# Reciprocal row sums spread by column strips of the array in place of row strips

## The chip, the cores and the metric

The kernel runs on one core of a Trainium2 chip. Its time is the device time in microseconds (us) of one launch; the time given for a kernel is the median of its runs. The engines of the core work side by side, each through its own queue in order: TensorE (PE; its weight loads are listed as PEld), VectorE (DVE), ScalarE (ACT), GpSimd (POOL) and SyncE (SP), which issues DMAs. The profile is one execution, recorded by the hardware.

TensorE multiplies a stationary operand of up to 128 rows by 128 columns (loaded by a weight load) with a moving one. In the profile a matmul's shape begins with the part of the array that it uses: `32*128` is a strip of 32 rows by all 128 columns (a row strip), `128*32` or `128*21` a strip of all rows by 32 columns (a column strip), `128*128` the full array.

## The reference

Four layers in a row, each a layer norm, an attention and a residual sum, on one sequence of 2048 rows of 640 numbers in bf16. There are 32 heads of 20. Layers 0 and 2 use weights A and look at a window of 256 rows; layers 1 and 3 use weights B and look at all rows.

```python
S, D, H, Dh, W = 2048, 640, 32, 20, 256
def attention(x, wqkv, wo, mask):
    q, k, v = split(x @ wqkv)                      # each 32 heads x 2048 x 20
    scores = einsum("bhqd,bhkd->bhqk", q, k) * Dh ** -0.5
    scores = where(mask, scores, -1e9)             # A: 0 <= i - j < 256; B: no mask
    o = einsum("bhqk,bhkd->bhqd", softmax(scores), v)
    return merge_heads(o) @ wo

x = A_x
x = x + A(layernorm(x)); x = x + B(layernorm(x))
x = x + A(layernorm(x)); x = x + B(layernorm(x))
```

## The kernel before

The rows are cut into four chunks of 512 queries, and the heads into eight groups of four. A *unit* is one layer, one chunk of queries and one group of four heads (layers 1 and 3 cut some units further by keys). Each head of a group lies on its own 32 partitions, 20 of which are used.

The main loop goes in ticks. In each tick TensorE computes up to three (at times four) banks of scores of 128 keys by 512 queries at L1326, from row strips, since each head has only 32 partitions; ScalarE takes the exponential of all of them in one instruction at L1357; and TensorE multiplies earlier exponentials with the values at L1387, from column strips: the four heads of a group write their 21 columns into four strips of 32 partitions. The 21st column of the values is one, so that the row sums of the softmax come out beside the results. Scores alternate between two sets of banks, so that TensorE writes one while ScalarE reads the other.

All other work (layer norm, projections, output products) is written as generators, which yield shares of cost. A planner (`pump`, `choose`, `advance`) advances them tick by tick, by the credit of the tick and by the unit that first needs their result; this happens when the program is built, so the order on each engine is fixed by the planner's costs and not by the times on the chip. Generators take one of two PSUM banks (`take_m`, `drop_m`), and when the planner reckons that TensorE has had too little to do in a tick (`cool`), it puts in matmuls whose result nobody reads (`unread`, `keep_clock`, `warm_bank`: groups of four of `ident` with `masks`, by column strips at L300). `by_columns` (L300) issues a product as four matmuls, one for each 32 columns of its stationary operand. The transposes of the layer norm at L437 have the same shape of 128 rows by 32 columns.

When a unit ends, its results and row sums are copied out of PSUM (L864), and units go in pairs into a *tail*, `t_tail`, which the planner prefers to all other work. The tail picks the row sums out with `sel4` (L300, 4 columns each), takes reciprocals (L1053), splits each into a high and a low bf16 part (L1057, L1058), transposes both (L1066) and copies them to `rT` (L1071), where a unit has 32 rows: 16 high and 16 low ones, one for each head and block of 128 queries. Then `scaled` spreads them for each unit: four matmuls (L1088), one for each block of 128 queries, whose stationary operand `spread4` has ones where a row belongs to a head. They use the 32 rows of the unit alone, the first unit's rows 0 to 31 and the second's 32 to 63, and all 128 columns. VectorE multiplies the unit's results by the spread (L1092), and with that the bank is free again. In the last tail `fill` adds matmuls of the full array (L1038). `rT` comes from a pool of three buffers; `spread4` is made once, on VectorE, in `other_constants` (L172 to L178).

Of the kernel before, what the change touches and what calls it, by code (L numbers as in the profile page):

```python
# [9 lines left out]
BF16 = mybir.dt.bfloat16  # L10
# [7 lines left out]
P = 128  # L18
# [30 lines left out]
def kernel(  # L49
# [10 lines left out]
    nc = tc.nc  # L60
# [3 lines left out]
    def pool(name, bufs, space=None):  # L64
        kw = {"space": space} if space else {}
        return ctx.enter_context(tc.tile_pool(name=name, bufs=bufs, **kw))

    big = pool("big", 1)
# [10 lines left out]
    rzp = pool("rzp", 3)  # L79
# [14 lines left out]
    ident = big.tile([P, P], BF16, name="ident", tag="ident")  # L94
    nhalf = big.tile([P, 4], F32, name="nhalf", tag="nhalf")
    sel4 = big.tile([P, 4], BF16, name="sel4", tag="sel4")
    spread4 = big.tile([64, 4, P], BF16, name="spread4", tag="spread4")
    masks = big.tile([P, 3, C], BF16, name="masks", tag="masks")

    kts = [big.tile([P, S], BF16, name=f"kt{n}", tag=f"kt{n}") for n in range(3)]  # L100
# [27 lines left out]
    def packed(l, c):  # L128

        return l == 3 and c > 0  # L130

    def load_wop(w, dense):
# [9 lines left out]
        out=ident[:], in_=ident[:], compare_op=ALU.not_equal, fill=1.0,  # L142
# [6 lines left out]
    for m, b, ge in (  # L149
# [6 lines left out]
            out=v, in_=v, compare_op=ALU.is_ge if ge else ALU.is_gt, fill=0.0,  # L156
# [5 lines left out]
    def other_constants():  # L162
        nc.vector.memset(op, 0.0)
        nc.vector.tensor_copy(
            out=sel4[:], in_=ident[:].rearrange("p (j m) -> p j m", j=4)[:, :, DH]
        )

        sp32 = rzp.tile([64, 2, 16], BF16, name="sp32", tag="sp32")
        sp16 = rzp.tile([64, 16], BF16, name="sp16", tag="sp16")
        for u in range(2):  # L170
            r = slice(32 * u, 32 * u + 32)
            nc.vector.tensor_copy(  # L172
                out=sp32[r], in_=ident[r, r].rearrange("p (n r) -> p n r", n=2)
            )
            nc.vector.tensor_tensor(
                out=sp16[r], in0=sp32[r, 0, :], in1=sp32[r, 1, :], op=ALU.add
            )
            nc.vector.tensor_copy(  # L178
                out=spread4[r].rearrange("p q (j m) -> p (q j) m", m=32),
                in_=sp16[r].unsqueeze(2).to_broadcast((32, 16, 32)),  # L180
            )

# [83 lines left out]
    def take_m():  # L266
        while True:
            b = min(mfree, key=mfree.get)
            if mfree[b][0] <= state["tick"]:
                mfree[b] = (1 << 30, 0)  # L270
                return b
            yield ("wait", 1)

    def drop_m(b):
        mseq[0] += 1
        mfree[b] = (state["tick"] + (not state["early"]), mseq[0])
# [19 lines left out]
    def by_columns(out_, lhsT, rhs, start, stop):  # L296

        for j in range(4):
            r = slice(32 * j, 32 * j + 32)
            nc.tensor.matmul(out_[r], lhsT=lhsT[:, r], rhs=rhs, start=start, stop=stop)  # L300
# [343 lines left out]
    def warm_bank(b):  # L644

        if cool() and (
            state["credit"] <= 0.0 or all(task.wake > state["tick"] for task in todo)
        ):
            unread(b)
# [382 lines left out]
    def t_tail(us):  # L1032
        final = us[-1][0:3] == (3, NC - 1, G - 1)

        def fill(count):

            for n in range(count * final):
                nc.tensor.matmul(  # L1038
                    ps[:, 0, :], lhsT=ident[:], rhs=masks[:, 0, :], start=True, stop=True
                )  # L1040

        n = len(us)
        yield ("wait", 2)
        fill(2)
        mb = yield from take_m()
        warm_bank(mb)
        zp = ps[:, mb, 0 : 16 * n]
        for i, (l, c, g, oT) in enumerate(us):
            for qb in range(4):
                a = 16 * i + 4 * qb  # L1050
                by_columns(zp[:, a : a + 4], oT[:, qb * P : (qb + 1) * P], sel4[:], True, True)
        rz = rzp.tile([P, 2, 16], F32, name="rz", tag="rz")[:, 0:n, :]
        nc.vector.reciprocal(out=rz.rearrange("p u r -> p (u r)"), in_=zp)  # L1053
        drop_m(mb)

        hl = rzp.tile([P, 2, 2, 16], BF16, name="hl", tag="hl")[:, 0:n]
        nc.vector.tensor_copy(out=hl[:, :, 0, :], in_=rz)  # L1057
        nc.vector.tensor_tensor(out=hl[:, :, 1, :], in0=rz, in1=hl[:, :, 0, :], op=ALU.subtract)  # L1058
        yield ("pe", 0.25)
        fill(3)  # L1060
        yield ("wait", 2)
        mb = yield from take_m()
        warm_bank(mb)
        rp = ps[0 : 32 * n, mb, :].bitcast(BF16)[:, 0:P]
        for i in range(n):
            nc.tensor.transpose(  # L1066
                out=rp[32 * i : 32 * i + 32], in_=hl[:, i].rearrange("p n r -> p (n r)"),
                identity=ident[:],
            )
        rT = rzp.tile([64, P], BF16, name="rT", tag="rT")  # L1070
        nc.vector.tensor_copy(out=rT[0 : 32 * n], in_=rp)  # L1071
        drop_m(mb)
        yield ("pe", 0.1)
        fill(1)
        yield ("wait", 2 if state["tick"] < last_tick[0] else 1)
        for i in range(n):
            yield from scaled(*us[i], 32 * i, rT, fill)
        if any(packed(l, c) for l, c, g, oT in us):
            yield ("wait", 2)
        for u in us:  # L1080
            yield from settle(*u)

    def scaled(l, c, g, oT, r, rT, fill):
        mb = yield from take_m()
        warm_bank(mb)
        zb = ps[:, mb, :]
        for qb in range(4):
            nc.tensor.matmul(  # L1088
                zb[:, qb * P : (qb + 1) * P], lhsT=spread4[r : r + 32, qb, :],
                rhs=rT[r : r + 32, :], start=True, stop=True,  # L1090
            )
        nc.vector.tensor_tensor(out=oT, in0=oT, in1=zb, op=ALU.mult)  # L1092
        drop_m(mb)
        yield ("pe", 0.3)
        fill(3)

    def settle(l, c, g, oT):
        on = ons[l, c]
        if packed(l, c) and not ((l, c) == (3, NC - 1) and g >= G - 2):
            for j in range(4):  # L1100
                r, a = (4 * g + j) * DH, 0
                while a < DH:
                    b, o = divmod(r + a, P)
                    n = min(DH - a, P - o)
                    nc.sync.dma_start(  # L1105
                        out=on[o : o + n, b, :], in_=oT[32 * j + a : 32 * j + a + n, :]
                    )
                    a += n
            if g == G - 1 or (l, c, g) == (3, NC - 1, G - 3):
                yield ("wait", 8)  # L1110
        ready.add(("tail", l, c, g))
        if (l, c, g) == (3, NC - 1, G - 3):
            push("before_last", t_before_last(), 0, 8.0)
        if g == G - 1:
            while any(("tail", l, c, n) not in ready for n in range(G)):
                yield ("wait", 1)
            need = first_use(l + 1, c, 0) if l < 3 else len(units) + c
            push(("out", l, c), t_out(l, c), need, 9.0)
            if l < 3:
                push_layer(l + 1, c)  # L1120
# [82 lines left out]
    with tc.manual_schedule():  # L1203
        first_ln()
        push_layer(0, 0)
        push("zeros", t_zeros(), 0, 0.0)
        require(("qk", 0, 0, 0))
        other_constants()

        def narrow(u):  # L1210
# [10 lines left out]
        while n < last_layer:  # L1221
            size = 2 if len(tiles) % 2 and narrow(banks[n][0]) else 3
            u = banks[n][0]
            at = placed.setdefault(id(u), [])
            extra = []
            if (
# [3 lines left out]
                kc, j = u.aside[len(at)]  # L1230
# [58 lines left out]
        while ended is None or t < ended + 8:  # L1289
# [3 lines left out]
            if t < len(tiles) or banks:  # L1293
# [9 lines left out]
                for b in cur:  # L1303
                    u = b[0]
# [18 lines left out]
                for n in range(2):  # L1323
                    for i, (u, j, m, b0, subs, first, last, end) in enumerate(cur):
                        for kc, q0, qn, col in subs[n : n + 1]:
                            nc.tensor.matmul(  # L1326
                                sp[:, i, col * P : (col + qn) * P],
                                lhsT=u.k(kc, j), rhs=u.q(j, q0, qn), start=True, stop=True,
# [22 lines left out]
                i = 0  # L1351
                while i < n_b:
                    b0 = cur[i][3]
                    k = i
                    while k < n_b and cur[k][3] == b0:
                        k += 1
                    nc.scalar.activation(  # L1357
                        out=pt[:, i:k, b0 * P :], in_=sp[:, i:k, b0 * P :],
                        func=ACT.Exp, scale=SCALE,
                    )  # L1360
                    i = k
# [9 lines left out]
            for n in range(2 if n_b == 0 or t > closed + 1 else 0):  # L1371
                u = pts[0][3][0] if pts else None
# [11 lines left out]
                for m, (kc, q0, qn, col) in enumerate(subs):  # L1384
                    for _, pg, i, b in group:
                        j = b[1]
                        nc.tensor.matmul(  # L1387
                            op[32 * j : 32 * j + VW, q0 * P : (q0 + qn) * P],
                            lhsT=u.v(kc, j), rhs=pg[:, i, col * P : (col + qn) * P],
                            start=(first and m == 0), stop=(last and m == len(subs) - 1),  # L1390
                            skip_group_check=u.windowed,
                        )
                if end and u.aside:
                    pair = side_done(u)
                    for n, (kc, j) in enumerate(u.aside):
                        nc.tensor.matmul(  # L1396
                            op[32 * j : 32 * j + VW, :], lhsT=u.v(kc, j),
                            rhs=pair[n // 2][:, n % 2, :], start=False,
                            stop=all(jj != j for _, jj in u.aside[n + 1 :]),
# [14 lines left out]
            if t > 0 and masked is not None:  # L1414
                cur_, pt_ = masked
                i = 0
                while i < len(cur_):
                    m, b0 = cur_[i][2:4]
# [4 lines left out]
                    for b in ((3,), (1, 2), (0,))[m] if split else ():  # L1423
                        if b < b0:
# [4 lines left out]
                            out=v, in_=v, compare_op=ALU.is_gt if later else ALU.is_ge, fill=0.0,  # L1429
# [3 lines left out]
                    if split and m != 1:  # L1433
# [5 lines left out]
                            out=pt_[:, i:k, cols], in0=pt_[:, i:k, cols], in1=mv_, op=ALU.mult  # L1439
                        )  # L1440
                    elif m is not None and not split:
# [5 lines left out]
                            out=pt_[:, i:k, cols], in0=pt_[:, i:k, cols], in1=mv_, op=ALU.mult  # L1447
                        )
                    i = k
# [36 lines left out]
```

## Time and profile before

| | |
|---|---|
| median of 3 runs | 2217.34 us (2212.51 to 2220.05) |
| the profiled execution's own time | 2218.73 us |
| its span, first to last instruction | 2217.0 us |
| mean granted clock of TensorE | 0.99 |
| busy: TensorE, ScalarE | 1930.9 us, 2140.9 us |
| busy: VectorE, POOL | 1201.2 us, 482.5 us |

A row of a group of instructions gives line, engine, operation, the tiles written and read, the shapes and the count; then, behind the first bar, the busy time in us and the mean time of one in ns; and behind the second the idle time of the engine just before them in us, with what ended most of it. A row of the timeline gives start and length in us, then engine, line and tiles; rows of the same kind that follow one another are merged, with their count, and idle time before them stands in brackets. A row of waits gives who waited for whom, the sum in us, the number of times and the longest. A row of a stretch of time gives its ends and length, then the busy time and count of instructions of PE, PEld, DVE, ACT and POOL, the mean granted clock, the share of the DMA engines and GB/s. The ends of matmuls are modelled, so that matmuls that run beside or close behind one another overlap in the rows; distances from start to start are the measure.

### The profile page before, as it was taken

How to read it: one execution, taken by the hardware profiler on the slowest of the kernel's cores; microseconds unless marked ns; L12 is line 12 of the kernel's file. 1: busy time of each engine (PE TensorE's matmuls, PEld its weight loads, DVE VectorE, ACT ScalarE, POOL GpSimd, SP SyncE). 2: the span in 40 equal slices, each digit the busy share in tenths (PEclk: the TensorE clock that was granted, in tenths of full speed). 3: DMA queues.
4: the chain of work that ended last, by engine and by line, in shares of the span. 5: the costliest groups of instructions: out<-in, count | busy, mean ns of one | idle time of the engine just before them, and what ended most of it. 6: DMA issues, size and time to landing. Idle time of an engine off the chain costs nothing. (4 is left out here: it accounts for less than half of the span.)

```text
span 2217.0 us, 70003 instructions
## 1 busy us (share of the span) xinstructions
PE 1930.9 (87%) x30367; PEld 748.9 (34%) x30367; DVE 1201.2 (54%) x2190; ACT 2140.9 (97%) x1733; POOL 482.5 (22%) x950
## 2 busy tenths in 40 slices
PE   8989999988889888888888988888888888888888
PEld 4444443433233333333333333332332222222223
DVE  6656564424445454544554533432477777777764
ACT  7889899999999999999999999999999999999997
POOL 6665445200131113401143112511000000000000
PEclk9999999999999999999999999999999999999999
DMA  6233233322210323112230123122221111111100
GB/s 200 74 93 94 80 88 92 91 80 50 78 46 23 80 60 91 37 36 66 66 102 26 40 80 97 38 59 62 61 58 31 33 35 41 32 32 43 44 20 17
DMA packets 88404, 137.09 MB, mean 62 GB/s; under 512 B 20766, under 2 KB 63486, under 8 KB 88094
## 3 DMA queue, kind: packets, MB, share of 16 engines
q1 hardware_dynamic: 68878, 79.43, 13.6%
q0 software_dynamic: 19216, 53.17, 8.2%
q8 instruction: 238, 3.90, 0.8%
q14 instruction: 72, 0.59, 0.1%
HBM read 99.52 MB, written 27.79 MB: 57 GB/s over the span
## 5 line engine op out<-in xcount | busy, mean ns | idle before, releaser
L1357 ACT ACTIVATE pt<-ps 128x1536 bf16<-128x1536 f32 (+2 forms) x1654 | 2101.8, 1461 | 41.6 <-PE ps L1326 30.3
L1326 PE MATMUL ps<-qt,kt 32*128 32x512 bf16 x3960 | 549.7, 385 | 90.8 <-ACT pt L1357 81.7
L300 PE MATMUL ps<-masks,ident 128*32 128x512 bf16 x5796 | 506.8, 387 | 116.4 <-ACT pt L1357 66.5
L1387 PE MATMUL ps<-pt,vt 128*21 128x512 bf16 x3900 | 397.8, 388 | 1.1 <-ACT pt L1357 1.1
L1326 PEld LDWEIGHTS <-kt 32*128 32x128 bf16 x3960 | 166.5, 91 | 495.6 <-issue 479.5
L300 PEld LDWEIGHTS <-ident 128*32 128x32 bf16 x5796 | 176.2, 94 | 297.4 <-issue 270.0
L1428 POOL TENSOR_SCALAR_AFFINE_SELECT pt<-pt 128x256 bf16<-128x256 bf16 (+2 forms) x505 | 214.3, 446 | 189.7 <-ACT pt L1357 183.7
L300 PE MATMUL ps<-xnT,wqk 128*32 128x512 bf16 x3320 | 224.7, 383 | 14.7 <-DVE rT L1071 3.5
L323 DVE CAST st<-ps 128x512 bf16<-128x512 f32 x134 | 92.7, 691 | 221.3 <-PE ps L300 216.9
L1387 PEld LDWEIGHTS <-vt 128*21 128x21 bf16 x3912 | 98.5, 89 | 253.0 <-issue 249.4
L920 DVE TENSOR_SCALAR xnT<-ps 128x512 int32<-128x512 f32 x136 | 93.5, 688 | 130.5 <-PE ps L914 120.7
L300 PE MATMUL ps<-wop,on 128*32 128x320 bf16 x3712 | 159.0, 300 | 5.9 <-DVE x_sb L568 3.5
L1438 DVE TENSOR_TENSOR pt<-pt,masks 128x512 bf16<-128x512 bf16 (+4 forms) x267 | 110.9, 431 | 94.3 <-ACT pt L1357 92.8
L300 PEld LDWEIGHTS <-on 128*32 128x32 bf16 x5760 | 119.7, 96 | 64.8 <-issue 31.1
L568 DVE TENSOR_TENSOR x_sb<-x_sb,ps 128x320 bf16<-128x320 bf16 x120 | 58.2, 485 | 147.3 <-PE ps L300 146.8
L1326 PE MATMUL ps<-qa,ka 32*128 32x384 bf16 (+2 forms) x1408 | 116.0, 276 | 23.5 <-ACT pt L1357 20.4
L300 PE MATMUL ps<-wv,xnT 128*32 128x320 bf16 x2560 | 115.0, 301 | 8.1 <-DVE on L1092 3.8
L300 PEld LDWEIGHTS <-wqk 128*32 128x32 bf16 x3320 | 83.8, 96 | 97.6 <-issue 41.4
L1092 DVE TENSOR_TENSOR on<-on,ps 128x512 bf16<-128x512 bf16 x128 | 86.3, 683 | 54.4 <-PE ps L1088 50.3
L864 DVE CAST on<-ps 128x512 bf16<-128x512 f32 x112 | 77.0, 688 | 58.7 <-PE ps L1396 31.1
L536 POOL DMA_DIRECT2D k_d<-st x75 | 43.0, 573 | 229.2 <-DVE st L323 217.5
L404 POOL TENSOR_SCALAR rstd<-mv 128x4 f32<-128x4 f32 x15 | 3.7, 248 | 384.6 <-DVE mv L391 376.4
(100 smaller groups left out, 1544.8 us busy)
## 6 DMA issues: line engine op xcount, KB each, us to landing
vt<-v_d SPq DMA_DIRECT2D x48, 336.0 KB
kt<-k_d SPq DMA_DIRECT2D x192, 80.0 KB
wqk<-in_B_wqkv_dram POOLq DMA_DIRECT2D x80, 160.0 KB, 3.4
wqk<-in_A_wqkv_dram POOLq DMA_DIRECT2D x70, 160.0 KB, 3.7
k_d<-st POOLq DMA_DIRECT2D x75, 128.0 KB, 2.5
q_d<-st POOLq DMA_DIRECT2D x75, 128.0 KB, 2.2
qt<-q_d SPq DMA_DIRECT2D x384, 20.0 KB
v_d<-vs POOLq DMA_DIRECT2D x16, 336.0 KB, 3.0
```

Of the source, the lines that this page charges most:

```text
L300: nc.tensor.matmul(out_[r], lhsT=lhsT[:, r], rhs=rhs, start=start, stop=stop)
L323: nc.vector.tensor_copy(out=out_, in_=in_)
L536: nc.gpsimd.dma_start(out=dst, in_=staging.pop())
L568: nc.vector.tensor_tensor(out=xv, in0=had, in1=yp, op=ALU.add)
L864: nc.vector.tensor_copy(out=oT, in_=op)
L920: V.tensor_scalar(out=xi.bitcast(I32)[:, i * C : (i + 1) * C], in0=side["psum"], scalar1=SCALE * LOG2E * FIX, scalar2=-127.0 * FIX, op0=AL ...
L1092: nc.vector.tensor_tensor(out=oT, in0=oT, in1=zb, op=ALU.mult)
L1326: nc.tensor.matmul(sp[:, i, col * P : (col + qn) * P], lhsT=u.k(kc, j), rhs=u.q(j, q0, qn), start=True, stop=True,)
L1357: nc.scalar.activation(out=pt[:, i:k, b0 * P :], in_=sp[:, i:k, b0 * P :], func=ACT.Exp, scale=SCALE,)
L1387: nc.tensor.matmul(op[32 * j : 32 * j + VW, q0 * P : (q0 + qn) * P], lhsT=u.v(kc, j), rhs=pg[:, i, col * P : (col + qn) * P], start=(first ...
L1428: nc.gpsimd.affine_select(out=v, in_=v, compare_op=ALU.is_gt if later else ALU.is_ge, fill=0.0, base=0, pattern=[[0, k - i], [-1 if later ...
L1438: nc.vector.tensor_tensor(out=pt_[:, i:k, cols], in0=pt_[:, i:k, cols], in1=mv_, op=ALU.mult)
```

## The change

The spread of the reciprocals over a unit's result goes through `by_columns`: for each block of 128 queries four matmuls of 128 rows by 32 columns stand in place of one of 32 rows by 128 columns. As all 128 rows take part, the table becomes `spread8`, one table of 128 rows for each of the two units of a tail with zeros outside the unit's own 32 rows, and the transposed reciprocals go into one of three slices of a lasting tile `rts` of 128 rows, whose lower half stays zero. POOL clears both once, ahead of VectorE's making of the table. The order of all other instructions on TensorE is the same.

```diff
-    spread4 = big.tile([64, 4, P], BF16, name="spread4", tag="spread4")
+    spread8 = big.tile([P, 2, 4, P], BF16, name="spread8", tag="spread8")
+    rts = big.tile([P, 3, P], BF16, name="rts", tag="rts")
...
+        nc.gpsimd.memset(spread8[:], 0.0)
+        nc.gpsimd.memset(rts[:], 0.0)
...
             nc.vector.tensor_copy(
-                out=spread4[r].rearrange("p q (j m) -> p (q j) m", m=32),
+                out=spread8[r, u].rearrange("p q (j m) -> p (q j) m", m=32),
                 in_=sp16[r].unsqueeze(2).to_broadcast((32, 16, 32)),
             )
...
-        rT = rzp.tile([64, P], BF16, name="rT", tag="rT")
+        rT = rts[:, rt_n[0] % 3, :]
+        rt_n[0] += 1
         nc.vector.tensor_copy(out=rT[0 : 32 * n], in_=rp)
...
-            yield from scaled(*us[i], 32 * i, rT, fill)
+            yield from scaled(*us[i], i, rT, fill)
...
-    def scaled(l, c, g, oT, r, rT, fill):
+    rt_n = [0]
+
+    def scaled(l, c, g, oT, i, rT, fill):
...
         for qb in range(4):
-            nc.tensor.matmul(
-                zb[:, qb * P : (qb + 1) * P], lhsT=spread4[r : r + 32, qb, :],
-                rhs=rT[r : r + 32, :], start=True, stop=True,
-            )
+            by_columns(zb[:, qb * P : (qb + 1) * P], spread8[:, i, qb, :], rT, True, True)
```

## The prediction

> **What bounds the kernel now.** I read the page's busy table first, then the groups of ScalarE's instructions before and after 420 us, then TensorE's waits in the later part.
>
> ```profile
> span 2217.0 us, 70003 instructions
> PE 1930.9 (87%) x30367; PEld 748.9 (34%) x30367; DVE 1201.2 (54%) x2190; ACT 2140.9 (97%) x1733; POOL 482.5 (22%) x950
> ```
> ```profile
> L1357 ACT ACTIVATE pt<-ps 128x1536 bf16<-128x1536 f32 (+5 forms) x306 | 335.2, 1163 | 28.8 <-PE ps L1326 21.3 <-issue 3.2 <-POOL pt L1428 3.0
> ...
> L1357 ACT ACTIVATE pt<-ps 128x1536 bf16<-128x1536 f32 (+3 forms) x1349 | 1768.0, 1529 | 13.4 <-PE ps L1326 9.6 <-POOL pt L1428 0.4 <-ACT pt L1357 0.2
> ```
> ```profile
> ACT pt L1357 <- PE ps L1326: 9.6, 21, 2.4
> ...
> PE ps L1326 <- ACT pt L1357: 91.2, 276, 0.8
> PE ps L300 <- ACT pt L1357: 66.5, 176, 0.9
> PE ps L300 <- DVE on L1092: 16.2, 40, 0.9
> ```
>
> ScalarE is busy 97% of the span, nearly all of it with the exponentials of L1357. The two middle rows are the stretches 0 to 420 us and 420 to 2217 us; the last fence is the later stretch alone. After 420 us ScalarE waits for the scores of L1326 for only 9.6 us in 21 waits, while TensorE waits for ScalarE 91.2 + 66.5 = 157.7 us. So TensorE, which the change touches, has room there: what it saves is worth at most the 9.6 us, and what it loses must first use up waits of 157.7 / 452 = 0.35 us each. Before 420 us the kernel is not so bound: ScalarE waits 21.3 us for L1326, and there TensorE's time can count.
>
> **The spread as it is.** Each of 128 units has four spread matmuls.
>
> ```profile
> L1088 PE MATMUL ps<-rT,spread x512: 211/214/225, 46.2 to 2209.5; 32*128 32x128 bf16 x171
> ```
> ```profile
> 2111.67 0.40 PE L300 MATMUL ps<-masks,ident 128*32 128x512 bf16 x4 [0.24 <-ACT pt L1357]
> 2112.00 0.39 PE L1326 MATMUL ps<-qt,kt 32*128 32x512 bf16 x3
> 2112.32 0.40 PE L1387 MATMUL ps<-pt,vt 128*21 128x512 bf16 x4
> 2112.54 0.39 PE L300 MATMUL ps<-masks,ident 128*32 128x512 bf16 x4
> 2112.86 0.39 PE L1088 MATMUL ps<-rT,spread 32*128 32x128 bf16 x4
> 2113.19 0.40 PE L300 MATMUL ps<-masks,ident 128*32 128x512 bf16 x4
> ```
>
> Here the price of changing the array's division stands: from L1387 to L300, both by column strips, it is 0.22 us from start to start, and from column strips to row strips or back (2111.67 to 2112.00, 2112.00 to 2112.32) 0.32 to 0.33. A change of division costs about 0.10 us. The four spreads take (0.39 - 0.21) / 3 = 0.06 us each, about 0.22 us together.
>
> **The change, part by part.**
>
> *Sixteen small matmuls for four.* Adds 1536 matmuls and 1536 weight loads. The nearest row with the new shape, weights of 128 rows by 32 columns and 128 moving columns, is the transposes of L437:
>
> ```profile
> 49.05 0.61 PE L300 MATMUL ps<-masks,ident 128*32 128x512 bf16 x8
> 49.50 0.45 PE L437 MATMUL ps<-ident,xn 128*32 128x128 bf16 x20
> ```
> ```profile
> L437 PE MATMUL ps<-ident,xn 128*32 128x128 bf16 x1200 | 28.9, 225 | 2.5 <-DVE xn L417 2.5
> L437 PEld LDWEIGHTS <-xn 128*32 128x32 bf16 x1200 | 23.9, 100 | 15.0 <-DVE xn L417 5.8 <-issue 1.3 <-DVE on L864 0.2
> ```
>
> Twenty of them are five rounds of four strips: (0.45 - 0.225) / 4 = 0.056 us a round, each with its own four loads. Four rounds of the new spread are therefore 0.22 us, as long as the four old ones. By themselves they cost nothing.
>
> The Trainium skill, "TensorE: Matmul & The Clock Gate", section "Part 3: Packing small matmuls", says that a weight load overlaps running matmuls only when its row group differs, and all sixteen new loads use all four row groups. By that rule each round would pay its load first. L437's rounds of 0.056 us, shorter than one load's 0.100, speak against it in this kernel.
>
> *Between column work on both sides* (42 units by the order in which TensorE's instructions are issued, the pair at 2112.54 to 2113.19 is one): masks to masks is 0.65 us now, and 0.22 + 0.22 = 0.44 with no change of division. TensorE saves 0.21, or 0.10 where the next matmul waits anyway. At most 42 x 0.21 = 8.8 us of TensorE's time.
>
> *After column work and before scores* (52 units after the first layer):
>
> ```profile
> 905.65 0.40 PE L300 MATMUL ps<-masks,ident 128*32 128x512 bf16 x4 [0.24 <-DVE on L1092]
> 905.98 0.23 PE L1088 MATMUL ps<-rT,spread 32*128 32x128 bf16 x1
> 906.01 0.39 PE L1326 MATMUL ps<-qt,kt 32*128 32x512 bf16 x2
> 906.05 0.33 PE L1088 MATMUL ps<-rT,spread 32*128 32x128 bf16 x3
> 906.22 0.37 PE L1326 MATMUL ps<-qt,kt 32*128 32x512 bf16 x1
> 906.52 0.40 PE L1387 MATMUL ps<-pt,vt 128*21 128x512 bf16 x4
> 907.16 0.40 PE L300 MATMUL ps<-xnT,wqk 128*32 128x512 bf16 x4 [0.24 <-DVE on L1092]
> ```
>
> Today the scores of other row strips run beside the spread (906.01), and only the score of the spread's own strip waits (906.22). Masks to L1387 is 0.87 us. Afterwards: 0.22 to the spread, 0.22 + 0.10 to the scores, 0.32 to L1387, sum 0.86. The overlap that is lost and the change of division that is moved cancel. Where no score shares the strip, the scores' end moves by up to +0.21, which the waits of 0.35 us cover; without that cover it would be 52 x 0.21 = 11 us.
>
> *The multiply after it.* In both groups the spread begins 0.10 us earlier, and so does VectorE's multiply of L1092, behind which TensorE waits for the bank (905.65, 907.16: a chain of 1.51 us a step). That is a gain where ScalarE is short of scores. The 20 waits that remain of the 21 without the longest (below) hold 9.6 - 2.4 = 7.2 us; 20 x 0.10 = -2.0 us is what I take, with 0 and -7.2 as its ends.
>
> *The first layer* (8 pairs of units after scores and before column work, 8 pairs before scores):
>
> ```profile
> 112.14 0.39 PE L1326 MATMUL ps<-qa,ka 32*128 32x384 bf16 x4
> 112.37 0.38 PE L1088 MATMUL ps<-rT,spread 32*128 32x128 bf16 x4
> 113.65 0.38 PE L1088 MATMUL ps<-rT,spread 32*128 32x128 bf16 x4 [0.89 <-ACT xnT L321]
> 114.42 0.62 PE L300 MATMUL ps<-masks,ident 128*32 128x512 bf16 x8 [0.40 <-DVE on L1092]
> ```
> ```profile
> 360.78 0.38 PE L1088 MATMUL ps<-rT,spread 32*128 32x128 bf16 x4
> 361.42 0.21 PE L1088 MATMUL ps<-rT,spread 32*128 32x128 bf16 x1 [0.25 <-DVE st L323]
> 361.43 0.33 PE L1326 MATMUL ps<-qa,ka 32*128 32x384 bf16 x2
> ```
>
> In the first kind the change of division moves ahead of the first spread: +0.10 a pair at most, often nothing, since the second waits for something else (0.89 for L321). In the second kind there are two changes more and the overlap of 361.43 goes: 0.20 + 0.22 = +0.42 a pair. On TensorE that is 8 x 0.10 + 8 x 0.42 = +4.2 us; ends 0 and +4.2. I take half, +2.1, because about half of these places have a wait of 0.25 us or more right behind.
>
> *Setup.* Two memsets on POOL, 1024 + 384 columns.
>
> ```profile
> L148 POOL MEMSET masks<- 128x1536 bf16 x1 | 1.4, 1378 | 0.0
> ```
> ```profile
> 10.71 0.24 POOL L465 MEMSET va<- 128x32 bf16 x1
> 16.85 0.90 POOL L1428 TENSOR_SCALAR_AFFINE_SELECT pt<-pt 128x384 bf16<-128x384 bf16 x1 [5.89 <-ACT pt L1357]
> ```
>
> 1408 / 1536 x 1.38 = 1.26 us, hidden in POOL's 5.89 us of idleness; without it +1.26. VectorE's copy into the table now waits for them. No DMA is added or moved, and the queues of SP and POOL keep their order. The copy into rT keeps its size, and the rotation over three slices replaces three buffers: 0. The last unit's spread stands between fills of the full array, where both kernels change division twice: 0, ends -0.1 and +0.1.
>
> **Sum.** -2.0 + 2.1 + 0 = +0.1 us on the profiled execution's 2218.73 us, which is 1.4 above the median of 2217.34. Against that median I forecast 2217.5 us, no change. The sum's own ends are -7.3 and +5.6 (with the 1.26): 2210 to 2223. A change within 0.3% (6.7 us) is one that a measurement of this kernel can't tell from none.
>
> **The rivals.**
>
> *Faster.* The spread's chain is on ScalarE's path more than I think, and the saved 0.10 to 0.21 us arrive. For this speaks that TensorE waits for L1092 in 40 places after 420 us. Against it, ScalarE's 9.6 us are all there is after 420 us. All 7.2 us gained and nothing lost early gives 2210; together with half-clock windows that vanish, 2207. It decides if ScalarE's waits for L1326 after 420 us fall under 3 us. Chance 0.16.
>
> *Slower, by the first layer and the clock.* Where TensorE waits long, the granted clock drops:
>
> ```profile
> 1279.19 2.96 ACT L1357 ACTIVATE pt<-ps 128x1536 bf16<-128x1536 f32 x2 [2.44 <-PE ps L1326]
> ```
> ```profile
> 0.00:420.00 420.00, 381.56 (x7398) 178.07 (x7398) 246.20 (x574) 368.95 (x382) 227.16 (x483) 0.97 0.36 100
> 1274.00:1281.00 7.00, 5.29 (x49) 1.70 (x49) 3.54 (x5) 4.50 (x5) 0.97 (x2) 0.76 0.51 156
> ```
>
> (The number before the last two is the clock.) One such place at 0.76 cost ScalarE 2.44 us. If the +4.2 us all count and shift waits in the first layer so that three more such drops come, it is 4.2 + 3 x 2.4 = +11.4, or 2229. It decides from two more drops on; without them 4.2 us stay inside 0.3%. For it speaks that the clock before 420 us is already only 0.97; against it, that TensorE gets more work there and not longer waits. Chance 0.18.
>
> *Slower, by weight loads that don't overlap.* This is the rule of the page named above, worked out here from rows: 4 rounds x 0.100 = +0.40 us a unit, 51 us on TensorE over 128 units. That is just above the mean wait of 0.35 us, so perhaps half would arrive: 2243. L437's rows speak against it. Chance 0.04.
>
> **How the numbers follow.** The remaining 0.62 is no change, so faster 0.16, same 0.62, slower 0.22. The range takes in the sum's ends and most of the first two rivals, 2207 to 2229; about 0.04 of the weight loads' case and the outer parts of the others stay out.
>
> **What would show it.** The changed profile should have 2048 spreads of 128*32, spaced 0.22 us from masks to spread and 0.22 from spread to masks; no scores beginning inside a spread; L1092 starting 0.1 us earlier behind column work; ScalarE's waits for scores after 420 us at 6 to 10 us; POOL's memsets at about 11 us with nobody behind them. Rounds of the spread longer than 0.1 us, ScalarE waits above 13 us after 420 us, or a clock under 0.96 before 420 us would make the forecast wrong.

## The result and the profile after

| | before | after |
|---|---|---|
| median of 20 runs each | 2217.48 us (2212.51 to 2222.93) | 2213.45 us (2207.86 to 2218.56) |
| ratio | | 0.9981, 95% interval 0.9974 to 0.9989 |
| the profiled execution, its span | 2218.73 us, 2217.0 us | 2214.57 us, 2212.8 us |
| mean granted clock of the profiled execution | 0.990 | 0.994 |

The change saves 4.0 us, 0.19%. That is inside the 0.3% that I called no change and inside the range, but the many runs tell it clearly from none, and the forecast of 2217.5 us was no change. In the changed kernel all lines from 178 on stand three or four lower (L1088 is now in L303, L1092 is L1095).

The page's head, the groups of ScalarE's exponentials before and after 420 us, and the waits after 420 us, all of the changed kernel:

```profile
span 2212.8 us, 73076 instructions
PE 1924.5 (87%) x31902; PEld 756.9 (34%) x31903; DVE 1201.3 (54%) x2190; ACT 2139.4 (97%) x1733; POOL 484.6 (22%) x952
```
```profile
L1360 ACT ACTIVATE pt<-ps 128x1536 bf16<-128x1536 f32 (+5 forms) x307 | 335.8, 1163 | 29.0 <-PE ps L1329 22.9 <-POOL pt L1431 3.0 <-issue 1.8
...
L1360 ACT ACTIVATE pt<-ps 128x1536 bf16<-128x1536 f32 (+3 forms) x1349 | 1767.0, 1535 | 13.8 <-PE ps L1329 10.8 <-POOL pt L1431 0.2 <-ACT pt L1360 0.2
```
```profile
PE ps L1329 <- ACT pt L1360: 93.9, 285, 0.8
PE ps L303 <- ACT pt L1360: 69.0, 184, 0.9
...
PE ps L303 <- DVE on L1095: 10.5, 24, 0.8
```

TensorE is busy 6.4 us less, and after 420 us it waits for the multiply 10.5 us in 24 places, where it waited 16.2 us in 40. ScalarE is busy for the same 97%. Its waits for scores after 420 us did not fall in this pair of executions (10.8 against 9.6 us): what the two executions differ in by chance is as large as what is looked for, so only many runs tell.

The spread now, between column work on both sides and then ahead of scores (the timeline of TensorE in the changed kernel):

```profile
2109.43 0.40 PE L1390 MATMUL ps<-pt,vt 128*21 128x512 bf16 x4
2109.66 0.39 PE L303 MATMUL ps<-masks,ident 128*32 128x512 bf16 x4
2109.87 0.40 PE L303 MATMUL ps<-rts,spread 128*32 128x128 bf16 x16
2110.12 0.40 PE L303 MATMUL ps<-masks,ident 128*32 128x512 bf16 x4
2110.45 0.39 PE L1329 MATMUL ps<-qt,kt 32*128 32x512 bf16 x3
```
```profile
903.52 0.40 PE L303 MATMUL ps<-masks,ident 128*32 128x512 bf16 x4
903.74 0.41 PE L303 MATMUL ps<-rts,spread 128*32 128x128 bf16 x16
904.08 0.39 PE L1329 MATMUL ps<-qt,kt 32*128 32x512 bf16 x3
904.40 0.40 PE L1390 MATMUL ps<-pt,vt 128*21 128x512 bf16 x4
904.93 0.40 PE L303 MATMUL ps<-masks,ident 128*32 128x512 bf16 x4
```

Masks to masks across the spread is 0.46 us; it was 0.65. Masks to L1390 with scores between is 0.88 us; it was 0.87. The same place before the change on TensorE's timeline, and the multiply on VectorE's before and after:

```profile
904.15 0.40 PE L300 MATMUL ps<-masks,ident 128*32 128x512 bf16 x4
904.48 0.39 PE L1088 MATMUL ps<-rT,spread 32*128 32x128 bf16 x4
```
```profile
904.91 0.69 DVE L1092 TENSOR_TENSOR on<-on,ps 128x512 bf16<-128x512 bf16 x1 [0.81 <-PE ps L1088]
```
```profile
904.19 0.69 DVE L1095 TENSOR_TENSOR on<-on,ps 128x512 bf16<-128x512 bf16 x1 [0.72 <-PE ps L303]
```

From masks to multiply it is 904.19 - 903.52 = 0.67 us; it was 904.91 - 904.15 = 0.76. The step of the chain, masks to masks, is 1.41 us where it was 1.50 (904.15 to the masks at 905.65 that the prediction shows). These are the distances that the prediction worked out, to 0.03 us.

### The profile page after: what moved, and what is told of

Same layout as the page of the kernel before. It is cut to its first block, busy times and chain, and to the rows that moved or that the text cites. A ratio compares the mean times of both kernels' runs of the same rounds, so it can differ in the third digit from the quotient of the medians.

```text
span 2212.8 us, 73076 instructions
## 1 busy us (share of the span) xinstructions
PE 1924.5 (87%) x31902; PEld 756.9 (34%) x31903; DVE 1201.3 (54%) x2190; ACT 2139.4 (97%) x1733; POOL 484.6 (22%) x952
## 5 line engine op out<-in xcount | busy, mean ns | idle before, releaser
L303 PE MATMUL ps<-masks,ident 128*32 128x512 bf16 x5796 | 504.9, 386 | 116.6 <-ACT pt L1360 69.0
L1390 PE MATMUL ps<-pt,vt 128*21 128x512 bf16 x3900 | 397.9, 387 | 2.2 <-ACT pt L1360 1.1
L303 PEld LDWEIGHTS <-ident 128*32 128x32 bf16 x5796 | 177.6, 94 | 294.7 <-issue 273.0
L303 PE MATMUL ps<-xnT,wqk 128*32 128x512 bf16 x3320 | 223.5, 382 | 13.8 <-DVE rts L1075 3.5
L1390 PEld LDWEIGHTS <-vt 128*21 128x21 bf16 x3912 | 98.6, 89 | 254.2 <-issue 250.8
L303 PE MATMUL ps<-wop,on 128*32 128x320 bf16 x3712 | 159.0, 300 | 5.3 <-DVE x_sb L571 3.5
L303 PEld LDWEIGHTS <-on 128*32 128x32 bf16 x5760 | 119.5, 95 | 64.2 <-issue 30.2
L303 PE MATMUL ps<-wv,xnT 128*32 128x320 bf16 x2560 | 115.0, 301 | 7.8 <-DVE on L1095 3.7
L303 PEld LDWEIGHTS <-wqk 128*32 128x32 bf16 x3320 | 83.6, 96 | 96.2 <-issue 40.5
L1095 DVE TENSOR_TENSOR on<-on,ps 128x512 bf16<-128x512 bf16 x128 | 86.4, 684 | 50.0 <-PE ps L303 48.9
```

The costliest lines, as they stand in the source:

```text
L1390: nc.tensor.matmul(op[32 * j : 32 * j + VW, q0 * P : (q0 + qn) * P], lhsT=u.v(kc, j), rhs=pg[:, i, col * P : (col + qn) * P], start=(first ...
```

## The experiments

All vary only `scaled`, how the spread is issued and what stands ahead of it, from the changed kernel's tables and slices. Every run here lists its span and mean granted clock. The same program's time follows that clock closely: over the 134 runs of the kernel before that were made beside the experiments, those at 0.990 mean 2219.9 us, those at 0.993 2216.6 and those at 0.996 2212.3. A line fitted to all 329 runs (one level for each kernel, one slope for all) falls 1.38 us for each 0.001 of clock and leaves a scatter of 1.45 us. So a kernel's difference splits into a part that goes with the clock and a part at equal clock, which is its work. Differences are to the mean of the kernel before, 2216.7 us at a clock of 0.9930 (means of all these runs, so that the changed kernel stands at -3.6 where the medians above give -4.0); the errors are standard errors.

| kernel | runs | mean us | difference | mean clock | at equal clock |
|---|---|---|---|---|---|
| before | 134 | 2216.7 | | 0.9930 ± 0.0002 | |
| changed kernel (first runs and e5) | 32 | 2213.1 | -3.6 | 0.9945 ± 0.0003 | -1.4 ± 0.3 |
| e1 columns in layers 1 to 3 | 12 | 2214.4 | -2.3 | 0.9931 ± 0.0004 | -2.1 ± 0.4 |
| e2, e13 columns in layer 0 | 24 | 2217.0 | +0.3 | 0.9933 ± 0.0005 | +0.7 ± 0.3 |
| e3 full array | 12 | 2217.0 | +0.3 | 0.9929 ± 0.0007 | +0.2 ± 0.4 |
| e4 rows in all layers | 12 | 2218.8 | +2.1 | 0.9919 ± 0.0004 | +0.7 ± 0.4 |
| e6 columns between columns | 11 | 2217.4 | +0.7 | 0.9922 ± 0.0004 | -0.4 ± 0.5 |
| e7 columns before scores | 12 | 2216.1 | -0.6 | 0.9934 ± 0.0006 | 0.0 ± 0.4 |
| e8 columns, spread twice | 11 | 2218.7 | +2.0 | 0.9956 ± 0.0004 | +5.7 ± 0.5 |
| e9 rows, spread twice | 12 | 2223.7 | +7.0 | 0.9946 ± 0.0004 | +9.3 ± 0.4 |
| e10 e1 with fills in layer 0 | 11 | 2213.5 | -3.1 | 0.9952 ± 0.0005 | -0.1 ± 0.5 |
| e11 changed, layer 0 twice | 12 | 2214.6 | -2.1 | 0.9947 ± 0.0003 | +0.2 ± 0.4 |
| e12 changed, no fill ahead | 12 | 2216.1 | -0.6 | 0.9924 ± 0.0005 | -1.3 ± 0.4 |
| e14 rows with fills in layer 0 | 11 | 2216.9 | +0.2 | 0.9939 ± 0.0003 | +1.6 ± 0.5 |
| e15 e1 with half of the fills | 11 | 2213.1 | -3.6 | 0.9946 ± 0.0004 | -1.3 ± 0.5 |

### Where the work is saved: e1, e2, e13

```diff
         for qb in range(4):
-            by_columns(zb[...], spread8[:, i, qb, :], rT, True, True)
+            if l > 0:      # e1; e2 and e13: l == 0
+                by_columns(zb[...], spread8[:, i, qb, :], rT, True, True)
+            else:          # row strips as before, out of the same tables
+                nc.tensor.matmul(zb[...], lhsT=spread8[32 * i : 32 * i + 32, i, qb, :],
+                                 rhs=rT[32 * i : 32 * i + 32, :], start=True, stop=True)
```

> Column strips for the 96 units of layers 1 to 3, row strips for the 32 units of layer 0 (table, slices and memsets as in the changed kernel). Theory 1 (the gain lies after layer 0, where the spread begins 0.10 us earlier behind column work, and layer 0 costs up to 4.2 us of TensorE, about 1 of it on ScalarE's path): a ratio to the kernel before of 0.9975, about 5.5 us faster. Theory 2 (the gain is the granted clock, which half-speed windows lower mostly before 420 us): most of the gain gone, ratio 0.9995. In either case ScalarE's waits before 420 us stay as in the kernel before, 28 us at L1357's line.

> Column strips for the 32 units of layer 0 only. Theory 1: 1 us slower than before, ratio 1.0005. Theory 2 (clock): ratio 0.9985, with fewer half-speed windows before 420 us than the kernel before had (mean clock there over 0.97).

> Column strips in layer 0 only, once more. Its first twelve runs had a mean clock of 0.9932 (error 0.0007) and stood 0.4 us over the kernel before at equal clock. If layer 0's columns make the changed kernel's clock of 0.9945, these runs lie at 0.9938 or more; if the clock needs the columns of all layers, at 0.9925 to 0.9935. Equal clock: 0 to 1 us over.

Ratios to the kernel before on the same chip: e1 0.9994 (0.9984 to 1.0004), e2 1.0001 (0.9990 to 1.0013), e13 1.0005 (0.9993 to 1.0016). Neither theory holds whole: e1's ratio is the 0.9995 of theory 2 and not the 0.9975 of theory 1, while e2 and e13 lie at the 1.0005 of theory 1 and not at the 0.9985 of theory 2. At equal clock the columns of layers 1 to 3 save 2.1 us and those of layer 0 cost 0.7; together -1.4, and the changed kernel, which has both, stands at -1.4. So the work adds up. Neither half has the changed kernel's clock.

### All rows at work, or the division: e3, e4

e3 issues four matmuls of all 128 rows by 128 columns (`lhsT=spread8[:, i, qb, :], rhs=rT`), e4 row strips for all units.

> Four matmuls a unit as before, but of all 128 rows by 128 columns of the same zero-filled tables. Theory 1 (changes of division and the start of the multiply): if the full array counts as a division of its own, the change stays on both sides of the spread and the scores can't run beside it: 0 to 0.3 us a unit lost on TensorE, ratio 1.0000 to 1.0010. Theory 2 (all rows at work lift the granted clock): ratio 0.998 as in the changed kernel.

> The changed kernel's tables, slices and memsets, but row strips for all 128 units, as before. Both theories: ratio 1.0000 within 0.0010; if the setup or the lasting tile matters, it shows here alone, up to 1.3 us either way.

Measured 1.0000 (0.9988 to 1.0012) and 1.0012 (1.0000 to 1.0023). The full array leaves time and clock as they were, so neither gain comes from the rows at work. Between column work it pays the change of division on both sides, as the row strips do (0.32 us to the spread and 0.32 to the next masks):

```profile
2108.36 0.39 PE L303 MATMUL ps<-masks,ident 128*32 128x512 bf16 x4
2108.68 0.40 PE L1099 MATMUL ps<-rts,spread 128*128 128x128 bf16 x4
2109.00 0.40 PE L303 MATMUL ps<-masks,ident 128*32 128x512 bf16 x4
```

e4's level at equal clock, +0.7 ± 0.4, leaves room for a small cost of setup and tile, but is not clear of none; its clock was the lowest of all. e4 shares tables, slices and memsets with every other experiment, so the parts can be counted from it as well: at equal clock e1 then stands at -2.7 ± 0.6, e2 and e13 at +0.1 ± 0.5 and the changed kernel at -2.1 ± 0.5. Which of the two is the right base rests on e4's twelve runs, which were not repeated.

### The changed kernel again, and its two kinds of places: e5, e6, e7

e5 is the changed kernel. e6 takes column strips for the 42 units between column work, e7 for the 52 before scores, by a list of the order in which the spreads are issued.

```diff
+        n_scaled[0] += 1
...
+            if n_scaled[0] in CC_UNITS:     # e7: CR_UNITS
                 by_columns(zb[...], spread8[:, i, qb, :], rT, True, True)
+            else:                           # row strips
```

> The changed kernel once more, on one chip with the runs beside it. Over all runs so far time falls 1.44 us for each 0.001 of mean granted clock; at equal clock the changed kernel stood 1.0 us under the kernel before, and its mean clock was 0.9946 against 0.9929. Theory 1a (the spread's columns lift the clock for good): mean clock again 0.9940 or more, 3 to 4 us under the kernel before. Theory 1b (the higher clock was chance of those runs, the work alone saves 1 to 2 us): mean clock 0.9925 to 0.9935 as the others, 1 to 2 us under.

> Column strips only for the 42 units whose spread stands between column work on both sides, row strips for all others. If the saved change of division is the gain: at equal clock all of it, 2 us under the kernel before (ratio 0.9991). If the earlier multiply is the gain, in proportion 42 of 94: 0.9 us.

> Column strips only for the 52 units of layers 1 to 3 whose spread stands before scores. If the saved change of division is the gain: none here, ratio 1.0000 at equal clock. If the earlier multiply is the gain, 52 of 94: 1.0 us under. If the lost overlap with the scores counts: up to 2 us over.

e5 gave 0.9983 (0.9972 to 0.9994) and a clock of 0.9943 in its own runs: the higher clock is the kernel's, theory 1a. e6 gave 1.0001 (0.9991 to 1.0010), e7 0.9998 (0.9988 to 1.0008). At equal clock -0.4 ± 0.5 and 0.0 ± 0.4: the sum of -0.4 ± 0.7 is less than e1's -2.1 ± 0.4, which has both. Counted from e4 it is -1.7 ± 1.0 against -2.7 ± 0.6, and the gap is no longer clear. So e6 misses its 2 us, and the saving can't be given to one kind of place. Fewer waits for the multiply did not pay by themselves either: in e7's profile TensorE waits for it 10.1 us in 22 places after 420 us, as little as in the changed kernel (10.5 in 24), and e7 shows no gain at equal clock. It may be that a pair of spreads, one of each kind in a tail, has to be shortened as a whole before it reaches ScalarE; that is argued, not shown.

### The price of TensorE's time: e8, e9

`for _ in range(2):` around the spread's matmuls, by columns (e8) and by rows (e9).

> The changed kernel with every spread issued twice into the same bank (32 small matmuls a unit): 0.22 us more of TensorE's work for each of 128 units, 28 us in all, and the multiply 0.22 us later. It prices TensorE's time around the spread: if ScalarE's bound hides it, 3 us or less over the changed kernel; if the tails lie on the path, 10 us or more. If busier TensorE lifts the clock, the mean clock is above the changed kernel's.

> Row strips for all units, each spread issued twice: 0.22 us more of TensorE's work a unit, as the doubled column strips had, but by row strips. Mean clocks so far: kernel before 0.9929, changed kernel 0.9945, doubled column strips 0.9956. If any work of TensorE in the tails lifts the clock, the mean clock is 0.9940 or more. If only work by columns does, it stays at 0.9920 to 0.9932. Time at equal clock: 3 to 7 us over the kernel before.

e8 against the kernel before 1.0011 (1.0002 to 1.0021), e9 1.0030 (1.0019 to 1.0041). The repeats in e8, as its profile counts the spread's instructions:

```profile
L303 PE MATMUL ps<-rts,spread x4096: 216/219/314, 46.3 to 2208.4; 128*32 128x128 bf16 x196
```

28 us more of TensorE's work (an estimate, 128 x 0.22 us) cost 7.2 us at equal clock over the changed kernel (e8), between the two cases expected, and 9.3 over the kernel before (e9), more than the 3 to 7 expected: a microsecond added to TensorE in the tails costs about 0.25 to 0.33 us. By this price the 4.2 us lost in layer 0 are 1.1 to 1.4, where e2 and e13 measured 0.7. The 8.8 us saved between column work, an upper end, would be worth 2.2 to 2.9 us; e1 measured 2.1, but e6, which saves just these, only 0.4 ± 0.5. So the price of added time doesn't carry over to saved time without more. And both lifted the clock, e9 by row strips as well, so columns are not needed for it; e3's full array, which also takes longer than the row strips where these ran side by side (0.62 us against 0.40 for a pair at 215 us), left it at 0.9929 ± 0.0007.

### Which work lifts the clock: e10, e11, e14, e15

e10 is e1 with four unread matmuls ahead of each of layer 0's spreads, e14 the same fills with row strips in all layers, e15 is e10 with the fill only ahead of the second spread of a pair. e11 is the changed kernel with layer 0's spreads twice.

```diff
         zb = ps[:, mb, :]
+        if l == 0:                 # e15: l == 0 and i == 1
+            by_columns(zb, ident, masks[:, 0, :], True, True)
```

> Column strips for layers 1 to 3; in layer 0 row strips, with four unread matmuls of 512 columns by column strips ahead of each of the 32 spreads (0.22 us each). Column strips for layers 1 to 3 alone had a mean clock of 0.9931. If the clock is lifted by work in layer 0's tails, it is 0.9940 or more here. Time at equal clock: up to 2 us over that kernel, since the spread starts later.

> The changed kernel with layer 0's 32 spreads issued twice. The doubled spreads of all units gave a mean clock of 0.9956 and cost 7 us at equal clock over the changed kernel. If layer 0 makes the clock: 0.9956 again, and 1 to 3 us over the changed kernel at equal clock. If all layers do: 0.9945 to 0.9950.

> Row strips in all layers, with four unread matmuls of 512 columns ahead of each of layer 0's 32 spreads. With columns in layers 1 to 3 the same fills had a clock of 0.9952. If work in layer 0's tails makes the clock by itself: 0.9945 or more, 2 to 3 us over the kernel before at equal clock. If not: about 0.993.

> Column strips in layers 1 to 3; in layer 0 row strips and the fill ahead of only the second spread of each pair, 16 in all. The fill ahead of all 32 gave a clock of 0.9952 and cost 2.1 us at equal clock over no fill. With half the fills: half the cost, 1.1 us under the kernel before at equal clock, and, if work in layer 0's tails makes the clock, 0.9942 to 0.9952, so 2212 to 2214 us, as fast as the changed kernel or 1 us faster.

Ratios: e10 0.9981 (0.9972 to 0.9990), e11 0.9989 (0.9978 to 1.0001), e14 1.0002 (0.9994 to 1.0011), e15 0.9984 (0.9976 to 0.9993). Fills in layer 0 lift the clock by 0.0021 ± 0.0007 where layers 1 to 3 have columns (e10 against e1) and by 0.0009 ± 0.0004 where they have rows (e14 against the kernel before; 0.0020 ± 0.0005 against e4). e14's clock lies between its two expected cases, and its +1.6 us at equal clock below the 2 to 3 expected; e10, e11 and e15 came out as one of their cases has it. The fills are not the change, but like it they give TensorE work in layer 0's tails. e11's clock is that of the changed kernel (0.9947): doubling layer 0's spreads alone did not bring e8's 0.9956. Its 32 x 0.22 = 7 us cost 1.7 ± 0.5 us at equal clock over the changed kernel, so in layer 0 too a microsecond is worth about a quarter. e15 is as fast as the changed kernel (2213.1 us both); none here is clearly faster.

At one place a difference of the clock can be seen. Layer 0 has a pair of spreads at 215 us, behind which TensorE waits for the multiply. Before and after:

```profile
215.08 0.39 PE L1326 MATMUL ps<-qa,ka 32*128 32x384 bf16 x4
215.30 0.40 PE L1088 MATMUL ps<-rT,spread 32*128 32x128 bf16 x8
217.43 0.61 PE L300 MATMUL ps<-masks,ident 128*32 128x512 bf16 x8 [1.73 <-DVE on L1092]
```
```profile
214.39 0.39 PE L1329 MATMUL ps<-qa,ka 32*128 32x384 bf16 x4
214.71 0.63 PE L303 MATMUL ps<-rts,spread 128*32 128x128 bf16 x32
216.74 0.61 PE L303 MATMUL ps<-masks,ident 128*32 128x512 bf16 x8 [1.40 <-DVE on L1095]
```

As row strips the two spreads ran beside one another and beside the scores (eight in 0.40 us), and TensorE then stood idle for 1.73 us. As column strips they take 0.63 us, and 1.40 us of idleness are left. The rows of the stretch 213 to 223 us, in which the number before the last two is the granted clock, of the kernel before, e1, the changed kernel, e5 and e10:

```profile
213.00:223.00 10.00, 7.92 (x152) 3.55 (x148) 7.32 (x18) 7.43 (x7) 5.58 (x12) 0.83 0.12 27
```
```profile
213.00:223.00 10.00, 7.91 (x152) 3.44 (x150) 7.33 (x19) 7.44 (x7) 5.59 (x12) 0.83 0.10 27
```
```profile
213.00:223.00 10.00, 8.25 (x225) 4.27 (x221) 8.16 (x19) 8.53 (x9) 5.59 (x12) 1.00 0.16 41
```
```profile
213.00:223.00 10.00, 8.26 (x214) 4.00 (x211) 8.13 (x20) 8.54 (x8) 5.57 (x12) 1.00 0.11 27
```
```profile
213.00:223.00 10.00, 9.00 (x189) 4.02 (x180) 8.54 (x22) 8.53 (x8) 5.17 (x12) 1.00 0.12 28
```

Within the stretch the kernel before stands at half speed, as this row of it shows:

```profile
219.00:220.00 1.00, 1.00 (x10) 0.24 (x10) 0.55 (x2) 1.00 (x1) 0.00 (x0) 0.50 0.00 0
```

0.83 over 10 us is a loss of 1.7 us, or 3.4 us at half speed. ScalarE (the fourth pair) does 7.43 us of work in these 10 us where the clock drops and 8.53 where it does not: 1.1 us for one drop. The line through all runs says the same: 1.7 of 2217 us is 0.0008 of the mean clock, and at 1.38 us for 0.001 that is 1.1 us. All six profiles of kernels with row strips and no fill in layer 0, e9's doubled ones among them, and that of the full array have 0.66 to 0.83 here; of the ten with column strips or fills there, seven have 1.00 and three (e12, e13, e15) 0.69 to 0.83. None of seven against seven of ten is more than chance would easily give, so what stands at the spread matters here; but the idle time behind it does not decide alone. The full array of e3 leaves the same 1.40 us as the column strips, and e9's doubled row strips only 1.29, and both have the drop (0.83 and 0.71):

```profile
215.06 0.62 PE L1099 MATMUL ps<-rts,spread 128*128 128x128 bf16 x8
217.09 0.98 PE L303 MATMUL ps<-masks,ident 128*32 128x512 bf16 x8 [1.40 <-DVE on L1103]
```
```profile
215.75 0.84 PE L1100 MATMUL ps<-rts,spread 32*128 32x128 bf16 x16
217.89 0.62 PE L303 MATMUL ps<-masks,ident 128*32 128x512 bf16 x4 [1.29 <-DVE on L1104]
```

What does decide is not shown. The Trainium skill ("TensorE: Matmul & The Clock Gate", section "Part 1: The HAM clock gate") says that TensorE's recent activity sets the granted clock. This place agrees in part: with columns or fills the drop stayed away in seven profiles of ten, while e3 and e9 gave TensorE more work there and had it.

It does not settle the whole 0.0015, of which one drop is 0.0008. In e2 and e13 layer 0 has the columns, and the mean clock is 0.9933 all the same; both their profiles have drops at about 1012, 1278, 1534 and 2082 us, all but the first of which the kernel before has as well. The changes of e1 (+0.0001 ± 0.0005) and of e2 and e13 (+0.0003 ± 0.0005) add up to 0.0004 ± 0.0007, against 0.0015 ± 0.0004 for the changed kernel: less, but not clearly. Counted from e4's clock of 0.9919 they do add up, 0.0012 + 0.0013 against 0.0026, each with an error of 0.0005 to 0.0006. Whether that low clock belongs to the setup or is chance was not tried. Which spreads lift the clock, and whether it takes both halves, stays open.

### The chain shortened further: e12

```diff
     def scaled(l, c, g, oT, i, rT, fill):
         mb = yield from take_m()
-        warm_bank(mb)
+        if l == 0:
+            warm_bank(mb)
```

> The changed kernel, but after layer 0 the planner puts no unread matmuls between a bank's release and the spread; it puts as many elsewhere in the tick. The spread and the multiply of L1092 begin about 0.22 us earlier in these 96 units, twice what the change itself brought. If the chain of spread, multiply and bank is what paid after layer 0: 2 to 4 us under the changed kernel at equal clock. If it is paid out already: the same within 1 us. The clock may fall if the fills land where TensorE is busy anyway.

0.9997 (0.9985 to 1.0010). At equal clock -1.3 ± 0.4, the same as the changed kernel: moving the fill out of the chain brought nothing more, so the earlier multiply is paid out already or was not what paid. The test is not complete: at the place at 903 us the first multiply does begin 0.21 us earlier behind L1390's matmuls, but from the first spread to the second it is 1.40 us (902.38 to 903.78 in e12), as in the changed kernel (903.74 to 905.15). The same number of fills (5796 matmuls in both profiles), placed elsewhere, gave a clock of 0.9924, and that took back 3 us against the changed kernel. So it matters to the clock where fills of the same number stand; why they did more ahead of the spreads was not tried.

## Why the prediction was wrong

*What held.* Four rounds of small matmuls take as long as four large ones (masks to masks 0.46 us, forecast 0.44). Weight loads of about 0.1 us before each round did not show, as L437's rows said. Between columns 0.19 us are saved (forecast 0.21); before scores the lost overlap and the moved change of division cancel (0.88 against 0.87); the multiply begins 0.09 us earlier (forecast 0.10). After layer 0 the work was forecast to bring -2.0 us: e1 measured -2.1 ± 0.4. That its mechanism is the multiply, as the forecast had it, is not shown, and the agreement may be luck: ScalarE's waits, from which the term was taken, did not fall (10.8 against 9.6 us), and e7 and e12 cut the waits for the multiply and show no gain from it. TensorE's saved time alone does not explain it either, as e6 shows.

*The setup.* It was put at 0; e4 allows that but is not clear of a small cost (+0.7 ± 0.4 us at equal clock). The memsets stand on POOL's timeline where they were put, and POOL still waits 5.27 us behind them:

```profile
10.60 0.95 POOL L169 MEMSET spread<- 128x1024 bf16 x1
11.49 0.42 POOL L170 MEMSET rts<- 128x384 bf16 x1
11.85 0.24 POOL L468 MEMSET va<- 128x32 bf16 x1
17.37 0.91 POOL L1431 TENSOR_SCALAR_AFFINE_SELECT pt<-pt 128x384 bf16<-128x384 bf16 x1 [5.27 <-ACT pt L1360]
```

*The first step that failed: the first layer at +2.1 us.* Its mechanism is there; the scores no longer run inside the spread, and the change of division stands ahead of it:

```profile
358.35 0.39 PE L1329 MATMUL ps<-qa,ka 32*128 32x384 bf16 x4
358.67 0.95 PE L303 MATMUL ps<-rts,spread 128*32 128x128 bf16 x32
359.55 0.33 PE L1329 MATMUL ps<-qa,ka 32*128 32x384 bf16 x2
```

Scores to spread is 0.32 us where it was 0.23 (360.55 to 360.78 before), and the scores at 359.55 wait for all of the second spread. But it costs 0.7 ± 0.3 us, not 2.1 (0.1 ± 0.5 counted from e4). I took half of TensorE's 4.2 us; the price of added time that e8, e9 and e11 measured is a quarter to a third, even in the layer where ScalarE waits most (e11). The reading that losses after layer 0 are free as long as waits of 0.35 us cover them does not hold either: e8 added 0.22 us to each unit and paid 7.2 us at equal clock, and 5.5 ± 0.6 of that after layer 0, since e11, which doubles layer 0's spreads alone, paid 1.7.

*The second step that failed: the sum had no term for the clock.* The granted clock appears in the prediction only as a rival that ends slower, with longer waits in layer 0. It went the other way, from 0.9930 to 0.9945, and 1.5 x 1.38 = 2.1 us of the 3.6 go with it. The sentence against that rival, that TensorE gets more work there and not longer waits, named the right sign, and it should have been carried on to a term of its own. That the clock rose is shown by both sets of the changed kernel's runs; why it rose stays open. At the place at 215 us both profiles of the changed kernel lack a drop that the kernel before has, but e3 and e9 filled the idle time there as much and had it. The rival's price of 2.44 us for a drop, the wait at one place, was too high as well: the place at 215 us and the line through all runs give 1.1. So -2.1 + 0.7 - 2.1 = -3.5 stands for the forecast's -2.0 + 2.1 + 0 = +0.1.

*The rivals.* Faster came true in direction, in part by a higher clock, as its last clause allowed, but not by ScalarE's waits for L1326 falling under 3 us after 420 us, which it named as its condition (10.8 us). The two slower ones did not come.

## What to carry to other kernels

On an engine that is off the critical path, added time costs a fraction that can be measured by doubling the piece of work: here 0.25 to 0.33 us for each microsecond of TensorE in the tails. Time saved need not bring as much, as e6 shows. Where the granted clock varies from run to run, list it with each run and compare at equal clock: a 1.4 us effect of the work and a 2.1 us effect of the clock came apart that way, while two single profiles could not show either. A change to TensorE's work in places where it waits can move the clock either way, so the forecast needs a term for it. An experiment that shares the changed kernel's setup but not its change (here e4) is the base for the parts, and deserves as many runs as the kernel before.

## What the runs showed of the hardware that was not expected

About four fifths of the variance of this kernel's times, 2209.8 to 2224.7 us in 134 runs, goes with TensorE's mean granted clock (correlation -0.89, squared 0.80), although ScalarE is the busy engine: a drop of 3.4 us to half speed at 215 us cost ScalarE 1.1 us. Changing the array's division costs 0.10 us (0.32 to 0.33 us from start to start against 0.22), to the full array too, and row strips of different rows, from unrelated parts of the program, run beside one another without any order to that effect: eight spreads of two units in 0.40 us. Issuing every spread twice by columns gave the highest mean clock here (0.9956 ± 0.0004, though e10's 0.9952 is not clearly lower), and a longer time all the same.
